# Blocks of 512 rows from the 40th pair on, beside the remaining convolution and routing

## The chip, the core and the metric

The kernel runs on one core of a Trainium2 chip. The metric is the device time of one execution in microseconds (us); less is better. The engines are TensorE (PE, with its weight loads PEld), VectorE (DVE), ScalarE (ACT), GpSimd (POOL) and SyncE (SP). SP and POOL only issue DMAs here, apart from some elementwise work on POOL.

## The reference

A causal convolution of seven taps, whose weights are a softmax per head, feeds a mixture of experts that picks one of eight experts for each row:

```python
w = softmax(weight)                               # 8 heads x 7 taps
y[b, s, c] = sum_k w[head(c), k] * x_padded[b, s + k, c]
logits = y @ w_gate                               # 8 experts
gate = sigmoid(y @ w_local)
for b in range(8):
    for s in range(3584):
        fresh = argmax(logits[b, s])
        e = fresh if s == 0 or gate[b, s] < 0.5 else prev
        prev = e
        p = softmax(logits[b, s])
        out[b, s] = p[e] * (relu(y[b, s] @ w1[e]) @ w2[e])
```

There are 8 x 3584 = 28,672 rows of 192 channels, 8 experts of 1024 hidden units, all in float32.

## The kernel before, in words

The rows are cut into 16 chunks of 1792 rows (`NPART`, `NT` = 14 rows on each of 128 partitions). For each chunk, side work runs in two generators:

- `conv` (L390): per head a first tap on ACT (L401) and six taps on DVE (L411), 8 first taps and 48 DVE instructions for a chunk. The next chunk's x is loaded in its middle.
- `route` (L625) with `logits` (L589): the convolved rows y are transposed on DVE in four instructions (L594), multiplied with the gate weights on PE (L604), copied out of PSUM by ACT (`ls`, L609), transposed back (`lq`, L612) and put in place by 16 small DVE copies (`lt`, L620). Then some seventy small DVE instructions find each row's expert, the probability (with one exp on ACT, L662) and the row's place in a sorted list; `tables` (L778) counts which blocks of 128 rows are full.

After routing, 14 indirect DMAs a chunk, issued by POOL in `put` (L794, the DMA is L801), scatter the rows of the chunk to `slots` in DRAM, sorted by expert. A row carries its probability and its index.

The main work goes over `blocks` (L918): a block is 1, 2 or 4 units of 128 rows of one expert. Before, there are 35 single blocks, 60 pairs (`PAIRED`), then, when all chunks are routed, 13 blocks of 512 rows ("quads"), 4 pairs and 14 singles; a few spare ones run only if they are needed. For each block SP loads the rows (L947) and the expert's weights (L940), three blocks ahead (`AHEAD`).

- A single or pair: `hidden` (L999) multiplies on PE, ACT applies the relu (L1004); `turn` transposes the next block's rows on PE (L383), ACT copies them to xT (L985); `output` multiplies (L1016), ACT scales one half (L1024), DVE adds the other (L1030), and POOL sends the rows out by an indirect DMA (L1034).
- A quad: `seven` (L1136) does the hidden product of 512 rows by 2 x 2 blocks in seven products in place of eight, and four more for the rest (L1152). Its sums are made by `combine_w` on POOL (L1115 to L1121), by `combine_x` on DVE (L1129 to L1133) and by three DVE additions out of PSUM (L1166, L1169, L1179). ACT copies products out of PSUM (L1158, L1161, L1163), applies relu (L1167, L1170, L1180, L1181) and copies the next rows (L1083). `output_late` then has two parts of 256 rows: products (L1196), ACT (L1206), DVE (L1209), POOL (L1214). [...]a quad uses [...]`xps` and three `late_p` tiles, which take the place of the tiles that singles and pairs use.

Every engine executes its instructions in the order in which this program writes them. The order of side work against blocks is set by hand: `step(time)` (L1258) takes instructions from the route and conv generators until their due costs (the numbers that they yield) reach `time`. "hop" ends routing for the step, so that the rest of it goes to the convolution. Steps stand at three places of a pair, with 4.8, 1.2 and 3.6; a quad has none. `ensure` (L1311) loads rows only when their chunk is routed and scattered, and forces steps when a block would come too early.

Of the kernel before, what the change touches and what calls it, by code (L numbers as in the profile page):

```python
# [17 lines left out]
P = 128  # L18
# [4 lines left out]
N = B * S  # L23
# [41 lines left out]
PAIRED = 60  # L65
LEFT4 = E * (QT // 2 + UT // 8)
LEFT2 = E * (BT // 2 + UT // 8)
# [3 lines left out]
PAST = ONE[-1] * UT + TWO[-1] * BT  # L71
FOUR = _likely(N - PAST, QT, LEFT4)
LOST = FOUR - _sure(N - PAST, QT)
# [7 lines left out]
REST = NU - ONE[-1] - 2 * TWO[-1] - 4 * FOUR - 2 * PAIRS + LOSE  # L81
# [21 lines left out]
def kernel(  # L103
# [14 lines left out]
    ys = ctx.enter_context(tc.tile_pool(name="ys", bufs=4))  # L118
# [5 lines left out]
    hp = ctx.enter_context(tc.tile_pool(name="hp", bufs=1))  # L124
    op = ctx.enter_context(tc.tile_pool(name="op", bufs=2))
# [244 lines left out]
    tab = [cst.tile([P, 3], F32, name=f"tab{k}") for k in range(5)]  # L370
    ends = [cst.tile([P, 1 + E], F32, name=f"ends{k}") for k in range(5)]
    for k in range(5):
        nc.gpsimd.memset(tab[k], 0.0)
        nc.gpsimd.memset(ends[k], 0.0)
# [12 lines left out]
    def row_tile():  # L387
        return ys.tile([P, NB, DG], F32, name="y_sb")

    def conv(g, x_sb):  # L390
        y_sb = row_tile()[:, :NT, :]
# [197 lines left out]
    def logits(g, y_sb):  # L589
# [6 lines left out]
        yield "hop"  # L596


        lps = [hps_p.tile([P, TQ * Q], F32, name="hps") for half in range(2)]
# [15 lines left out]
        for r in range(4):  # L615
            for j in range(4):
                t, u = TQ * j, min(TQ * (j + 1), NT)
                at = r // 2 * TQ + t - begin[j]
                e0 = r % 2 * (E + 1)
                nc.vector.tensor_copy(lt[Q * r:Q * r + Q, t:u, :],  # L620
                                      lq[Q * j:Q * j + Q, at:at + u - t, e0:e0 + E + 1])
                yield 0.12
        return lt

    def route(g):  # L625
# [62 lines left out]
        krow = sm.tile([1, 2, P], F32, name="krow")  # L688
# [89 lines left out]
    def tables(g):  # L778
        if ONE[g] > (ONE[g - 1] if g else 0):
            yield from table(0, g, 1, ONE[g])  # L780
        if TWO[g] > (TWO[g - 1] if g else 0):
            yield from table(1, g, 2, TWO[g])
        if g == LAST:
            yield from table(2, g, 4, FOUR, 0)
            yield from table(3, g, 2, PAIRS, 0)
            yield from table(4, g, 1, None)
            yield from fill(g)
# [133 lines left out]
    blocks += [(2, 4, i, LAST) for i in range(FOUR)]  # L921
    blocks += [(3, 2, i, LAST) for i in range(PAIRS)]
    blocks += [(4, 1, i, PADS) for i in range(REST)]
# [40 lines left out]
    def turn(n, xg):  # L964
# [9 lines left out]
        xT = tp.tile([P, KD, BT], F32, name="xT")  # L974
# [69 lines left out]
    def ring(i):  # L1044

        if "rows" not in room:
            room["rows"] = row_tile().rearrange("p b d -> p (b d)")
# [3 lines left out]
    def make_room():  # L1051

        one, two = [xs.tile([P, NX, D], F32, name="x_sb").rearrange("p t d -> p (t d)")
                    for _ in range(2)]
        three = row_tile().rearrange("p b d -> p (b d)")
        for name, flat, at, size in (("xT", one, 0, KD * QT), ("xc", one, KD * QT, 4 * HU * P),
                                     ("wt", one, KD * QT + 4 * HU * P, 6 * P),
                                     ("h0", two, 0, 4 * HU * P), ("h1", two, 4 * HU * P, 4 * HU * P),
                                     ("h2", two, 8 * HU * P, 4 * HU * P), ("h3", three, 0, 4 * HU * P)):
            room[name] = flat[:, at:at + size]  # L1060
# [13 lines left out]
    def turn_in(n, at):  # L1074
        xT = room["xT"][:, :KD * n * P].rearrange("p (d s) -> p d s", d=KD)
# [34 lines left out]
    def combine_w(wb):  # L1110


        wt = room["wt"].rearrange("p (k s) -> p k s", k=3)
        b11, b12, b21, b22 = [wb[:, k * 2 * P:(k + 1) * 2 * P] for k in range(4)]
        nc.gpsimd.tensor_tensor(wt[:, 1, :], b22, b12, op=Alu.subtract)  # L1115
# [3 lines left out]
        nc.gpsimd.tensor_tensor(wt[:, 0, :], b22, b12, op=Alu.subtract)  # L1119
        yield  # L1120
        nc.gpsimd.tensor_tensor(wt[:, 2, :], b21, wt[:, 0, :], op=Alu.subtract)  # L1121
        yield wt

    def combine_x(xT):


        xc = room["xc"].rearrange("p (k s) -> p k s", k=4)
        one, two = slice(0, HU * P), slice(HU * P, KQ * P)
        nc.vector.tensor_tensor(xc[:, 0, :], xT[:, 0, one], xT[:, 0, two], op=Alu.subtract)  # L1129
        nc.vector.tensor_tensor(xT[:, 0, two], xT[:, 0, two], xT[:, 1, two], op=Alu.add)  # L1130
        nc.vector.tensor_tensor(xc[:, 1, :], xT[:, 0, two], xT[:, 0, one], op=Alu.subtract)
        nc.vector.tensor_tensor(xc[:, 2, :], xT[:, 1, one], xc[:, 1, :], op=Alu.subtract)
        nc.vector.tensor_tensor(xc[:, 3, :], xT[:, 2, one], xT[:, 2, two], op=Alu.subtract)  # L1133
        return xc

    def seven(wb, wt, xT, xc, turn_next, weights_next):  # L1136
# [5 lines left out]
        t2, t3, t4 = [wt[:, k, :] for k in range(3)]  # L1142
        a11, s1, a12, a22, a13, a23 = [xT[:, d, s] for d in range(KD) for s in (one, two)]
        s3, s2, s4, s5 = [xc[:, k, :] for k in range(4)]
# [20 lines left out]
        times(wbk, a13, b31)  # L1165
        nc.vector.tensor_tensor(h11, wbk, h11, op=Alu.add)  # L1166
# [17 lines left out]
    def output_late(n, wb, xg, hT, rows_next=None, between=None):  # L1184

        for part, h in enumerate(hT):
# [18 lines left out]
            for k in range(m):  # L1205
                nc.scalar.activation(o_sb[:, k, :], yps[:, 0, k * D:(k + 1) * D], Act.Copy,  # L1206
                                     scale=xg[:, at + k, 0:1])
            for k in range(m):
# [18 lines left out]
    st = {"block": 0, "conv": 1, "cgen": None, "route": 1, "rgen": None, "routed": 1}  # L1227
# [30 lines left out]
    def step(time):  # L1258
# [3 lines left out]
        go = st["rgen"] is not None  # L1262
        while time > 0:
            c = route_op() if go else conv_op()
            if c is None:
                if not go:
                    break
                go = False
            elif c == "hop":
# [3 lines left out]
            else:  # L1273
                time -= c

    ya, yb = row_tile(), row_tile()
    hot = cst.tile([P, 2, NB, UT], F32, name="hot")
# [232 lines left out]
```

## Time and profile before

| | us |
|---|---|
| median of three runs | 1331.99 (1330.92 to 1332.77) |
| the profiled execution's own time | 1305.35 |
| its span, first to last instruction | 1303.6 |
| PE busy | 1284.2 |
| DVE busy | 846.3 |
| ACT busy | 651.1 |
| POOL busy | 523.1 |
| mean granted TensorE clock | 0.997 |

The profile describes one execution; the other times are of executions without it. In the profile a row gives the source line, the engine, the operation, output and inputs by the program's names, and the time that the engine sat idle ahead of it, with what ended that idle time. A name can be that of a tile whose memory was taken over: in quads, `x_sb` and `y_sb` hold hidden values and sums, and block rows.

By its stages the span is: up to about 252 us the start and the singles, then the 60 pairs, from 911 us the 13 quads, from 1176 us the last pairs and singles.

### The profile page before, as it was taken

How to read it: one execution, taken by the hardware profiler on the slowest of the kernel's cores; microseconds unless marked ns; L12 is line 12 of the kernel's file. 1: busy time of each engine (PE TensorE's matmuls, PEld its weight loads, DVE VectorE, ACT ScalarE, POOL GpSimd, SP SyncE). 2: the span in 40 equal slices, each digit the busy share in tenths (PEclk: the TensorE clock that was granted, in tenths of full speed). 3: DMA queues.
4: the chain of work that ended last, by engine and by line, in shares of the span. 5: the costliest groups of instructions: out<-in, count | busy, mean ns of one | idle time of the engine just before them, and what ended most of it. 6: DMA issues, size and time to landing. Idle time of an engine off the chain costs nothing.

```text
span 1303.6 us, 40830 instructions
## 1 busy us (share of the span) xinstructions
PE 1284.2 (99%) x16434; PEld 1220.6 (94%) x16434; DVE 846.3 (65%) x2526; ACT 651.1 (50%) x1482; POOL 523.1 (40%) x577
## 2 busy tenths in 40 slices
PE   9899999999999999999999999999999999999997
PEld 7799999999999999999999999999999999999997
DVE  5989898988988899998999996801333333330000
ACT  5456565544445445444454544444645556454453
POOL 3455353533435344353544534454433433322211
PEclk9999999999999999999999999999999999999999
DMA  5799999975757576575765755666323323324584
GB/s 195 285 357 415 386 384 345 398 273 202 269 203 278 196 274 244 207 280 190 281 246 204 281 193 205 214 213 235 128 87 135 122 105 140 110 94 167 212 303 164
DMA packets 63077, 300.42 MB, mean 230 GB/s; under 512 B 12064, under 2 KB 34263, under 8 KB 45474
## 3 DMA queue, kind: packets, MB, share of 16 engines
q1 hardware_dynamic: 40560, 252.54, 53.2%
q0 software_dynamic: 22320, 45.22, 9.5%
q8 instruction: 131, 2.15, 0.7%
q14 instruction: 64, 0.52, 0.1%
q10 hardware_dynamic: 2, 0.00, 0.0%
HBM read 252.12 MB, written 46.07 MB: 229 GB/s over the span
## 4 chain that ended last, share of the span: by engine, by line
PE 96%; DVE 3%; issue 0%; POOL 0%; POOLq 0%; ACT 0%; DVEq 0%
PE yps L1016 31%; PE hps L999 31%; PE ps L1196 15%; PE ps L1152 8%; PE ps L1103 4%; PE xps L383 2%; PE xps L1152 2%; PE hps L604 2%; DVE y_sb L411 1%; PE hps L233 1%; PE hps L178 0%; DVE hot L574 0%; PE hps L256 0%; PE yps L264 0%; DVE run L475 0%
## 5 line engine op out<-in xcount | busy, mean ns | idle before, releaser
L1016 PE MATMUL yps<-wb,hT 64*128 64x192 f32 x4960 | 429.8, 325 | 3.2 <-DVE o_sb L1030 2.4
L999 PE MATMUL hps<-xT,wb 64*128 64x256 f32 (+1 forms) x4560 | 425.9, 338 | 1.9 <-DVE at L503 1.2
L999 PEld LDWEIGHTS hps<-xT,wb 64*128 64x128 f32 x4560 | 378.7, 188 | 33.9 <-issue 3.9
L1016 PEld LDWEIGHTS yps<-wb,hT 64*128 64x128 f32 x4960 | 405.7, 187 | 4.6 <-DVE o_sb L1030 2.7
L411 DVE SCALAR_TENSOR_TENSOR y_sb<-x_sb,c,y_sb 128x336 f32<-128x336 f32 x672 | 375.6, 569 | 28.4 <-ACT y_sb L401 10.5
L801 POOL DMA_INDIRECT slots<-y_sb,posi x228 | 229.6, 1007 | 205.7 <-ACT xT L985 90.8
L1004 ACT ACTIVATE hT<-hps 128x512 f32<-128x512 f32 (+1 forms) x380 | 176.4, 516 | 244.5 <-PE hps L999 244.5
L1034 POOL DMA_INDIRECT out_dram<-o_sb,xg x155 | 161.5, 1042 | 276.0 <-DVE o_sb L1030 222.2
L1209 DVE SCALAR_TENSOR_TENSOR o_sb<-ps,y_sb,o_sb 128x192 f32<-128x192 f32 x74 | 28.1, 413 | 233.5 <-ACT o_sb L1206 233.5
L1214 POOL DMA_INDIRECT out_dram<-o_sb,y_sb x74 | 76.4, 1032 | 237.5 <-DVE o_sb L1209 218.7
L1196 PE MATMUL ps<-wb,x_sb 64*128 64x192 f32 x1952 | 165.0, 323 | 0.0
L1196 PEld LDWEIGHTS ps<-wb,x_sb 64*128 64x128 f32 x1952 | 159.3, 187 | 0.6
L1024 ACT ACTIVATE o_sb<-yps,xg 128x192 f32<-128x192 f32 x155 | 58.7, 418 | 178.4 <-PE yps L1016 178.3
L985 ACT COPY xT<-xps 128x256 f32<-128x256 f32 (+3 forms) x380 | 142.0, 374 | 10.6 <-PE xps L383 4.8
L1030 DVE SCALAR_TENSOR_TENSOR o_sb<-yps,xg,o_sb 128x192 f32<-128x192 f32 x155 | 58.6, 410 | 77.2 <-ACT o_sb L1024 77.0
L1206 ACT ACTIVATE o_sb<-ps,y_sb 128x192 f32<-128x192 f32 x74 | 27.9, 418 | 102.2 <-PE ps L1196 97.7
L1152 PE MATMUL ps<-x_sb,wb 64*128 64x256 f32 x624 | 73.7, 376 | 0.0
L1152 PEld LDWEIGHTS ps<-x_sb,wb 64*128 64x128 f32 x624 | 59.0, 187 | 7.3
L401 ACT ACTIVATE y_sb<-x_sb,c 128x336 f32<-128x336 f32 x112 | 61.9, 578 | 0.0
L1103 PE MATMUL ps<-x_sb,wb 64*128 64x128 f32 (+1 forms) x864 | 61.6, 295 | 0.0
L1103 PEld LDWEIGHTS ps<-x_sb,wb 64*128 64x128 f32 x864 | 59.4, 188 | 0.9 <-issue 0.2
L1083 ACT COPY x_sb<-xps 128x128 f32<-128x128 f32 (+5 forms) x124 | 58.7, 473 | 2.3
(277 smaller groups left out, 1043.5 us busy)
## 6 DMA issues: line engine op xcount, KB each, us to landing
wb<-in_w_dram SPq DMA_DIRECT2D x122, 1536.0 KB
x_sb<-in_x_dram SPq DMA_DIRECT2D x14, 1920.0 KB
xg<-slots SPq DMA_DIRECT2D x60, 195.0 KB
wb<-in_w_dram SPq DMA_DIRECT2D x12, 512.0 KB
y_sb<-slots SPq DMA_DIRECT2D x13, 390.0 KB
slots<-y_sb,posi POOLq DMA_INDIRECT x228
xg<-slots SPq DMA_DIRECT2D x33, 97.5 KB
x_sb<-in_xb_dram SPq DMA_DIRECT2D x4, 768.0 KB
```

The lines of the kernel that those rows point to most:

```text
L401: nc.scalar.activation(cols(h), chans(h, 0), Act.Copy, scale=c[:, h, 0:1])
L411: nc.vector.scalar_tensor_tensor(cols(h), chans(h, k), c[:, h, k:k + 1], cols(h), Alu.mult, Alu.add)
L801: ins = nc.gpsimd.indirect_dma_start(out=slots[:, :], in_=rows, in_offset=None, out_offset=bass.IndirectOffsetOnAxis(ap=to, axis=0)).ins
L985: copied = nc.scalar.copy(a, b)
L999: nc.tensor.matmul(hps[half][:, j, w], lhsT=wb[rows, f0:f0 + P], rhs=xT[rows, d, w], start=(d == 0 and j == 0), stop=(d == KD - 1), skip_g ...
L1004: relu = nc.scalar.activation(hT[:, m:m + 2, w], hps[half][:, :, w], Act.Relu)
L1016: nc.tensor.matmul(yps[half][:, k * D:(k + 1) * D], lhsT=hT[rows, m, k * P:(k + 1) * P], rhs=wb[rows, WA + m * D:WA + (m + 1) * D], start= ...
L1034: sent = nc.gpsimd.indirect_dma_start(out=out, in_=o_sb[:, k, :], in_offset=None, out_offset=bass.IndirectOffsetOnAxis(ap=xg.bitcast(I32)[ ...
L1103: nc.tensor.matmul(hps[:, half, j, :], lhsT=wb[rows, f0:f0 + P], rhs=xT[rows, d, :], start=(d == 0 and j == 0), stop=(d == KD - 1), skip_g ...
L1152: ins = nc.tensor.matmul(to[:, half, j, :], lhsT=b[rows, j * P:(j + 1) * P], rhs=a[rows, :], start=(first and j == 0), stop=True, skip_gro ...
L1196: ins = nc.tensor.matmul(yps[:, half, k * D:(k + 1) * D], lhsT=h[two][rows, side, j, k * P:(k + 1) * P], rhs=wb[rows, WA + f * D:WA + (f + ...
L1214: sent = nc.gpsimd.indirect_dma_start(out=out, in_=o_sb[:, k, :], in_offset=None, out_offset=bass.IndirectOffsetOnAxis(ap=xg.bitcast(I32)[ ...
```

## The change

Quads begin after the 40th pair. From there on, 18 quads are planned while chunks are still being convolved and routed (`MID`), 5 more come after the last chunk, so there are 35 singles, 40 pairs, 23 quads, 4 pairs and 14 singles. Side work stands in a quad in four parts (`SIDE`): before the first DVE addition (2.4), after the copies of the next rows (4.6) and in the two parts of the output (1.7 and 1.5), between ACT's and DVE's step. What a part overran is taken from the next (`over`), and each routing instruction counts 0.05 more there. The logits products of a chunk, marked by "pe", are written in the first output part of a quad, with a `late_p` tile as PSUM. The 16 small copies `lt` go from DVE to ACT, four to a step.

Memory is dealt out anew, since conv needs its tiles in the stage of quads: hidden values lie in `hot`, small sums in row tiles `xg` and in `hT`; the y tiles of chunk 8 and later rotate over three buffers, and the fourth holds the rows of quads. `combine_x` of the first quad is split, its last two instructions follow the last pair's output. Scatters may also be issued in the second output part of a quad.

```diff
-PAIRED = 60
+NARROW = 8
+PAIRED = 40
 LEFT4 = E * (QT // 2 + UT // 8)
+LEFTM = E * (QT // 2 + UT // 2)
...
+MID = [_likely((g + 1) * PT - PAST, QT, LEFTM) if TWO[g] == TWO[-1] else 0
+       for g in range(LAST)]
...
-    def row_tile():
-        return ys.tile([P, NB, DG], F32, name="y_sb")
+    def row_tile(g):
+        at = g % 4 if g < NARROW else (g + 1) % 3
+        return ys[at].tile([P, NB, DG], F32, name="y_sb")
...
-        yield "hop"
-        lps = [hps_p.tile([P, TQ * Q], F32, name="hps") for half in range(2)]
+        yield "pe"
+        if late_p:
+            both = st["bank"].tile([P, 2, 512], F32, name="ps")
+            lps = [both[:, half, :TQ * Q] for half in range(2)]
+        else:
+            lps = [hps_p.tile([P, TQ * Q], F32, name="hps") for half in range(2)]
...
-                nc.vector.tensor_copy(lt[Q * r:Q * r + Q, t:u, :],
-                                      lq[Q * j:Q * j + Q, at:at + u - t, e0:e0 + E + 1])
-                yield 0.12
+                nc.scalar.copy(lt[Q * r:Q * r + Q, t:u, :],
+                               lq[Q * j:Q * j + Q, at:at + u - t, e0:e0 + E + 1])
+            yield "hop"
...
+        if MID[g] > (MID[g - 1] if g else 0):
+            yield from table(2, g, 4, MID[g], MID[g - 1])
...
+    blocks += [(2, 4, i, next(g for g in range(NPART) if i < MID[g])) for i in range(MID[-1])]
+    blocks += [(3, 4, i, LAST) for i in range(FOUR)]
...
@@ seven @@
         times(wbk, a13, b31)
+        if st["block"] > FIRST:
+            step(SIDE[0], early=1)
         nc.vector.tensor_tensor(h11, wbk, h11, op=Alu.add)
...
@@ output_late @@
+            if n == KQ:
+                step(SIDE[2 + part], late_p[0] if part == 0 else None)
...
+    SIDE = (2.4, 4.6, 1.7, 1.5)
...
-    def step(time):
+    def step(time, bank=None, early=0, force=False):
         start_route()
         start_conv()
         go = st["rgen"] is not None
+        if st["due"]:
+            go = not late_p or bank is not None and (force or st["since"] < st["block"])
+            if go:
+                st["due"], st["bank"] = False, bank
+        time += st["over"]
         while time > 0:
...
+            elif c == "pe":
+                st["due"], st["since"], go = True, st["block"] - early, False
...
-                time -= c
+                time -= c + 0.05 if go and late_p else c
+        st["over"] = min(time, 0) if late_p else 0
...
@@ the main loop @@
                 xc = combine_x(xT)
+                next(xc)
             step(2.4 if i == 0 else 2.1 if n == 1 else 4.8)
             output(n, wbs.pop(i), xgs.pop(i), hT)
...
+            if i == FIRST - 1:
+                more_room()
+                xc = next(xc)
+            if i < FIRST - 1:
+                step(1.3 if n == 1 else 3.6)
...
         if n_next:
             xT, _ = turn_in(n_next, at)
+        if n == KQ:
+            step(SIDE[1])
```

## The prediction, made before the run

> **What bounds the kernel now.** I first read the share of each engine (part 1 of the page), then the stage table. Its columns after the stretch are its length, then busy time of PE, weight loads, DVE, ACT and POOL, then clock, DMA share, GB/s.
>
> ```profile
> PE 1284.2 (99%) x16434; PEld 1220.6 (94%) x16434; DVE 846.3 (65%) x2526; ACT 651.1 (50%) x1482; POOL 523.1 (40%) x577
> ```
> ```profile
> 252.00:911.00 659.00, 659.00 (x8220) 619.35 (x8207) 530.71 (x1680) 313.76 (x711) 289.74 (x284) 1.00 0.67 236
> 911.00:1176.00 265.00, 265.00 (x3010) 249.84 (x3008) 89.08 (x151) 144.58 (x196) 93.24 (x103) 1.00 0.33 115
> ```
>
> PE has no idle time in the stretch of pairs (252 to 911) nor in that of 512-row blocks, "quads" below (911 to 1176). So only less PE work, or a new PE wait, moves the end. Then the chain of waits, which gives the length of a block: start, duration, what.
>
> ```profile
> 846.17 5.18 PE hps L999 x48
> ...
> 899.50 5.18 PE hps L999 x48
> 905.15 5.26 PE yps L1016 x64
> 910.40 3.45 PE ps L1152 x32
> 920.42 10.40 PE ps L1196 x128
> 930.82 3.45 PE ps L1152 x32
> ...
> 1175.62 5.18 PE ps L1103 x48
> ```
>
> Five pairs lie from 846.17 to 899.50: 53.33/5 = 10.67 us each. Thirteen quads lie from 910.40 to 1175.62: 265.22/13 = 20.40 us each. A quad does 11 block products where two pairs do 12; its price is additions on DVE and POOL.
>
> Last, the timeline of one quad (it starts on PE at 1053.16) and of the change from pairs to quads, for the slack of what a quad waits for.
>
> ```profile
> 1054.30 1.01 ACT L1158 COPY x_sb<-ps 128x1024 f32<-128x1024 f32 x1 [0.18 <-PE ps L1152]
> 1055.76 1.03 PE L1152 MATMUL ps<-x_sb 64*128 64x256 f32 x8
> 1058.63 1.23 DVE L1166 TENSOR_TENSOR x_sb<-xps,x_sb 128x1024 f32<-128x1024 f32 x1 [3.74 <-PE xps L1152]
> 1059.77 1.21 DVE L1169 TENSOR_TENSOR y_sb<-ps,y_sb 128x1024 f32<-128x1024 f32 x1
> 1061.40 1.08 PE L1152 MATMUL ps<-x_sb 64*128 64x256 f32 x8
> ```
> ```profile
> 907.87 0.73 POOL L1117 TENSOR_TENSOR wb<-wb 128x256 f32<-128x256 f32 x1
> 907.94 0.94 DVE L1130 TENSOR_TENSOR x_sb<-x_sb 128x256 f32<-128x256 f32 x1 [1.21 <-ACT x_sb L1083]
> 908.92 0.83 DVE L1131 TENSOR_TENSOR x_sb<-x_sb 128x256 f32<-128x256 f32 x1
> 910.24 2.75 PE L1152 MATMUL ps<-x_sb,wb 64*128 64x256 f32 x24
> ```
>
> The copy L1158 ends at 1055.31 and the product that overwrites its PSUM starts at 1055.76: slack 0.45 us. The add L1169 ends at 1060.98, the product into its PSUM starts at 1061.40: slack 0.42 us. DVE waits 3.74 us before L1166; that is where side work must fit.
>
> **What the Trainium skill says.** "SBUF — State Buffer", section "Who interferes with whom": a DVE instruction with two SBUF inputs contends with a GpSimd instruction that reads SBUF. The trace agrees: L1130 and L1131, 0.42 us in their median, took 0.94 and 0.83 us beside the POOL subtractions. "ScalarE: Activation LUTs", section "What ACT_TABLE_LOAD costs": an ACTIVATE takes 186 ns + 0.833 ns per element with immediate operands. The trace agrees roughly (L1158, 1024 elements from PSUM: 1039 ns by this, 1012 measured). No page bears on the rest.
>
> **The change, part by part.**
>
> *Twenty pairs become ten quads.* The table counts agree: 60 pairs and 13 quads before, 40 and 23 after, all else alike. 10 x (2 x 10.67 - 20.40) = 9.3 us less PE work. This is the whole gain.
>
> *Small copies of logits.* 224 copies (L620, mean 190 ns, 42.6 us) leave DVE. On ACT I price one at 186 + 0.833 x 36 = 216 ns by the skill, 48 us in all. In the pairs this gains nothing: PE is full there, 659.00 of 659.00. It costs nothing while ACT's idle 345 us (659 - 314) cover it; a group of four (0.9 us, one per step) stands ahead of the relu L1004, which has over 1 us before L1016 wants it. If the copies had to wait for a late transpose L612, PE could lose up to 1 us per chunk, 12 us in the twelve chunks routed there; I take 0, since L612 follows L609 within 0.6 us in the chunks that I looked at, and keep the 12 for the range. A gain below nothing is excluded by the full PE, apart from the first 250 us, where PE idles for reasons ahead of the first copies.
>
> *Side work beside quads.* By the order of the built program, chunks 14 and 15 are convolved and 13 to 15 routed in blocks 75 to 90; thirteen of these quads carry 8 us or more. A quad's own DVE work is 89.08/13 = 6.9 us of 20.4, the parts allow 10.2, and four POOL subtractions that hit two-input DVE instructions add some 4 x 0.45 = 1.8: 18.9, so it fits in sum. In place, counted from the quad's PE start: the previous output's DVE step L1209 ends at 1.7, the first part (2.4) runs to 4.1, and L1166 can start at 5.47: 1.4 us spare. From L1179's end at 9.2 the second part (4.6) runs to 13.9, with three collisions 15.2; the third (1.7) to 16.9, against 16.0 for L1209; L1209, the five combine_x instructions and the fourth collision end at 20.2, the last part (1.5) at 21.8, L1209 at 22.5 and the next first part at 24.9, before the next L1166 at 25.9. Products want the combine_x results from 21.3. So about 1 us is spare even with every collision, and I take 0.6 us in all for what comes late all the same (a convolution that starts behind ACT's xT copies, exp read by DVE). Bounds: 0, and 1 us in each of thirteen quads.
>
> *ACT in a quad.* The last part's ACT instructions are queued behind the second L1206 and ahead of L1158. L1206 ends at 0.95, L1158 wants 1.14 and has 0.45 us of slack, so 0.6 us is free. One first tap (L401, 0.58) passes. By the built order, the first quad's last part issues four copies and a tap: 0.9 + 0.58 = 1.44, so 0.8 us late on PE; two later ones issue four copies: 0.2 to 0.3 each. I take 1.2 us.
>
> *The change from pairs to quads.* Before, no side work was left there and PE ran on from 905.15 + 5.26 to 910.40 without a gap. Now chunk 13's transposes (L594, 3 x 0.935 + 0.53 = 3.3 us) are queued on DVE behind the first three combine_x instructions, which wait for ACT's xT copies, and its logits products L604 stand on PE right behind the last pair's output. Taken from the trace before, L1131 ends at 909.75; plus 3.3 is 913.05, where PE would be free at 910.24: 2.8 us of PE wait. Also new: the quad's first PSUM tile lies over the tiles of these logits, so PE waits for the two ls copies L609 (0.43 with some 0.2 of latency): 0.6 us. Sum 3.4; bounds 0 (if the transposes run earlier than I think) and 5.
>
> *Moved buffers and queues.* y tiles of chunk 8 and later rotate over three buffers: the first tap on ACT waits for the scatters of the chunk three earlier, with relu L1004 queued behind it. In the built order the last of these scatters is issued about one block (10.7 us) ahead, so 0; up to 1 us if POOL lags. POOL gets scatters beside quads: 7.2 us per quad plus at most ten of 1.0 us, under 20.4, and the subtractions among them are due a quad later. SP: row and weight loads still go out three blocks ahead, none is forced; the x loads of the last chunk now fall beside quads, where the DMA share is 0.33. Cost 0.
>
> Sum: -9.3 + 3.4 + 1.2 + 0.6 = -4.1 us. Against the profiled execution (1305.35 us; its span is 1303.6) that is 1301.2. The shown runs have median 1331.99, 26.6 us above the profiled time, for which the profile has no place; I put the difference on the median: 1327.9.
>
> **Rivals.** (1) *The gain comes whole*: PE runs through the change of stage and the copies are hidden. For it: DVE has spare time in the sum; against it: the order of the queues at the change. -9.3 to -7: 1322.7 to 1325. (2) *DVE becomes the bound of the loaded quads, slower*: the place is L1166/L1169, of which the latter has 0.42 us. If collisions and the small routing instructions put these adds about 1.4 us late, each of thirteen quads loses 1 us: -9.3 + 3.4 + 13 = +7, 1339. It loses against before from 5.9/13 = 0.45 us per quad. For it: L1130 at 0.94 in place of 0.42; against it: 1 us spare after all collisions, and lateness is carried into the next budget. (3) *The pairs pay for ACT's copies*: a late L612 holds the relu and then PE, in twelve chunks by some 0.35 us: 4 us, so no change: 1331.9.
>
> **Chances.** Forecast 0.55, rival (1) 0.20, (2) 0.15, (3) 0.10. About 0.2% (2.7 us) can be told from no change. The forecast's own range is 1325 to 1330.5; four fifths of it (0.44) and all of (1) are faster: 0.64. Same: 0.11 + 0.10 and 0.03 of (2): 0.24. Slower: 0.12. The range from 1322.5 to 1334.5 leaves out most of (2).
>
> **What would show it.** In the profile after: quads of 20.4 us; a PE gap near 3 us ahead of the first quad with DVE L594's successor as releaser; small PE gaps behind L1158's successor; pairs still at 10.67 and no PE idle there. I am wrong if loaded quads run over 20.9 us, if the chunk period of the pairs grows from 55.05 us (first blocks of two chunks at 428.53 and 483.58 in the chain), or if no gap stands at the change.

## The result, and the profile after

The changed kernel took 1340.81 us (median of 7 runs, 1336.93 to 1344.37) against 1331.99 us for the kernel before (7 runs, 1330.92 to 1333.61): ratio 1.0065, 95% interval 1.0046 to 1.0084, slower by 0.65%. The forecast was 1327.9 us. The profiled execution of the changed kernel took 1337.14 us, with a span of 1335.4 us at a granted clock of 0.997.

One fact has to stand ahead of every comparison. In the five comparisons below, the kernel before, unchanged, takes 1305 us in two and 1324 to 1332 us in three, at granted clocks of 0.99 to 1.00 in all of them. The record numbers their chips 15, 14, 8, 13 and 13. The two with number 13 lie twelve minutes apart and have 1331.99 and 1324.67 us for the same kernel, so "a 1305 us chip" below means a chip as it was in one comparison; whether a chip is always quick or slow is not shown. The profile of before that the prediction uses is one of a 1305 us chip: run again on such a chip (run e0_before) it repeats itself stage by stage, and on a 1332 us chip (run d1_before) it does not. The profile of the changed kernel below is one of a slower chip. So the two profiles may not be subtracted; each comparison below stays on one chip or says that it doesn't.

Lines have moved: L999, L1016 and L1004 of before are now L1016, L1033 and L1021; L594, L604, L609, L612, L620 are L603, L617, L622, L625, L633; L1152 is L1173, L1158 is L1179, L1166 and L1169 are L1189 and L1192.

The answer to the first lines shown of before: the share of each engine, and the stretches of singles, of pairs and of quads (columns as in the prediction).

```profile
PE 1294.8 (97%) x16354; PEld 1242.9 (93%) x16354; DVE 890.6 (67%) x2457; ACT 723.9 (54%) x1656; POOL 555.3 (42%) x619
```
```profile
46.00:271.00 225.00, 211.14 (x3325) 201.03 (x3324) 186.55 (x532) 126.96 (x413) 94.64 (x96) 1.00 0.91 346
271.00:726.00 455.00, 447.95 (x5583) 425.98 (x5580) 377.95 (x1130) 243.98 (x609) 191.53 (x188) 1.00 0.67 239
726.00:1206.00 480.00, 475.05 (x5514) 461.28 (x5516) 285.91 (x665) 274.52 (x412) 225.84 (x240) 1.00 0.36 126
...
```

TensorE has 80 matmuls less to do, as planned, but pairs and quads are no longer full: in the profile of before neither had any idle time, now it is 7 us in the pairs and 5 in the quads. The list of waits (engine, line, what it waited for; total us, times, longest) names them:

```profile
PE yps L1033 <- issue: 5.2, 11, 0.9
PE hps L617 <- issue: 4.3, 13, 0.4
PE ps L1173 <- ACT hot L1184: 4.2, 3, 2.4
PE yps L1033 <- ACT hT L1021: 2.4, 4, 1.3
...
PE hps L1016 <- issue: 2.1, 7, 0.5
PE hps L617 <- DVE z L603: 2.1, 3, 1.3
```

Three kinds are seen: gaps that the profile gives no releaser ("issue"; the releaser is what ended the wait), waits for ScalarE (a relu in singles, the copy L1184 in quads), and the wait for the transposes z ahead of the first quad. The last one in the timeline:

```profile
719.32 0.83 DVE L1151 TENSOR_TENSOR xg<-xT 128x256 f32<-128x256 f32 x1
...
720.08 3.14 DVE L603 STREAM_TRANSPOSE z<-y_sb 128x768 f32<-128x768 f32 x4
...
721.19 0.41 PE L617 MATMUL hps<-z,wg 64*32 64x128 f32 x4 [1.29 <-DVE z L603]
...
721.95 0.41 PE L617 MATMUL hps<-z,wg 64*32 64x128 f32 x4 [0.36 <-DVE z L603]
...
722.81 2.72 PE L617 MATMUL hps<-z,wg 64*32 64x128 f32 x88 [0.45 <-DVE z L603]
...
725.56 0.43 ACT L622 COPY ls<-hps 128x128 f32<-128x128 f32 x2 [4.95 <-PE hps L617]
...
726.04 3.44 PE L1173 MATMUL ps<-xT,wb 64*128 64x256 f32 x24 [0.51 <-ACT ls L622]
```

The transposes start where the third addition ends, the logits products follow them one by one, and the first quad waits for the `ls` copy: the order and the releasers that the prediction gave. The second quad shows the other place that it named, small copies and a first tap on ScalarE ahead of L1179:

```profile
748.12 0.90 ACT L633 COPY lt<-lq 32x36 f32<-32x36 f32 x4
749.03 0.58 ACT L410 ACTIVATE y_sb<-x_sb,c 128x336 f32<-128x336 f32 x1
749.52 0.99 ACT L1179 COPY hot<-ps 128x1024 f32<-128x1024 f32 x1
...
750.60 1.14 PE L1173 MATMUL ps<-xg 64*128 64x256 f32 x8 [0.70 <-issue]
```

### The profile page after: what moved, and what is told of

Its sections match the earlier page's. It is cut to its first block, busy times and chain, and to the rows that moved or that the text cites. A ratio compares the mean times of both kernels' runs of the same rounds, so it can differ in the third digit from the quotient of the medians.

```text
span 1335.4 us, 40770 instructions
## 1 busy us (share of the span) xinstructions
PE 1294.8 (97%) x16354; PEld 1242.9 (93%) x16354; DVE 890.6 (67%) x2457; ACT 723.9 (54%) x1656; POOL 555.3 (42%) x619
## 5 line engine op out<-in xcount | busy, mean ns | idle before, releaser
L1033 PE MATMUL yps<-wb,hT 64*128 64x192 f32 x3680 | 328.3, 326 | 10.2 <-issue 5.2
L1016 PE MATMUL hps<-xT,wb 64*128 64x256 f32 (+1 forms) x3600 | 325.2, 329 | 3.7 <-issue 2.1
L1033 PEld LDWEIGHTS yps<-wb,hT 64*128 64x128 f32 x3680 | 304.6, 187 | 17.1 <-issue 11.0
L1016 PEld LDWEIGHTS hps<-xT,wb 64*128 64x128 f32 x3600 | 298.6, 188 | 19.5 <-issue 5.1
L1219 PE MATMUL ps<-wb,hot 64*128 64x192 f32 x3648 | 305.8, 323 | 0.0
L1219 PEld LDWEIGHTS ps<-wb,hot 64*128 64x128 f32 x3648 | 298.4, 187 | 1.2 <-issue 0.8
L1021 ACT ACTIVATE hT<-hps 128x512 f32<-128x512 f32 (+1 forms) x300 | 132.7, 495 | 155.7 <-PE hps L1016 81.4
L1002 ACT COPY xT<-xps 64x256 f32<-64x256 f32 (+4 forms) x300 | 108.1, 360 | 14.9 <-remote 6.7
L1173 PE MATMUL ps<-xT,wb 64*128 64x256 f32 x736 | 88.5, 378 | 0.5 <-ACT ls L622 0.5
L1103 ACT COPY xT<-xps 64x512 f32<-64x512 f32 (+6 forms) x164 | 86.0, 525 | 2.3
L1173 PEld LDWEIGHTS ps<-xT,wb 64*128 64x128 f32 x736 | 75.2, 188 | 4.3 <-ACT ls L622 1.0
L1189 DVE TENSOR_TENSOR hot<-xps,hot 128x1024 f32<-128x1024 f32 x23 | 28.2, 1224 | 59.7 <-PE xps L1173 57.0
L1123 PE MATMUL ps<-xT,wb 64*128 64x128 f32 (+1 forms) x864 | 61.6, 295 | 0.5 <-ACT o_sb L1229 0.5
```

Source lines behind the costliest of these rows:

```text
L1002: copied = nc.scalar.copy(a, b)
L1016: nc.tensor.matmul(hps[half][:, j, w], lhsT=wb[rows, f0:f0 + P], rhs=xT[rows, d, w], start=(d == 0 and j == 0), stop=(d == KD - 1), skip_g ...
L1021: relu = nc.scalar.activation(hT[:, m:m + 2, w], hps[half][:, :, w], Act.Relu)
L1033: nc.tensor.matmul(yps[half][:, k * D:(k + 1) * D], lhsT=hT[rows, m, k * P:(k + 1) * P], rhs=wb[rows, WA + m * D:WA + (m + 1) * D], start= ...
L1103: copied = nc.scalar.copy(a, b)
L1173: ins = nc.tensor.matmul(to[:, half, j, :], lhsT=b[rows, j * P:(j + 1) * P], rhs=a[rows, :], start=(first and j == 0), stop=True, skip_gro ...
```

## The stages on two kinds of chip

Each length is the difference of two starts on TensorE, read in the timeline: the first product L1016 (L999 before), the first of them 256 columns wide (first pair), the first L1173 (L1152), the first L1123 behind the last quad, and the end of the last product.

| execution | singles | pairs | quads | rest |
|---|---|---|---|---|
| before, the profile of the prediction | 207.85 | 657.71 | 265.20 | 119.04 |
| before, e0_before (1305 us chip) | 207.00 | 657.95 | 265.20 | 119.45 |
| changed, a1_after (1305 us chip) | 211.11 | 445.30 | 474.48 | 119.80 |
| before, d1_before (1332 us chip) | 222.49 | 669.26 | 265.40 | 121.53 |
| changed, d2_after (1332 us chip) | 224.15 | 456.65 | 479.44 | 120.16 |
| changed, the profile of the result | 225.51 | 454.72 | 480.47 | 119.80 |

The quads of before, which have no side work, take the same time on both chips. The quads of the changed kernel take 4 to 6 us more on the slower ones; its last eight take 20.2 to 20.5 there too (20.42 in six of them), so the loss lies in those with side work.

## The experiments

There are five comparisons, each on one chip. Theory 1 put the loss at the start of the quads and inside them; theory 2 put it on the small copies on ScalarE, which hold the relu and so TensorE.

**First comparison (before: 1305.43 us).** e0_before is the kernel before.

> The kernel before, unchanged, profiled once more. Theory A (the profiled execution of before, 1305 us, was quicker than its usual 1332, and the waits named 'issue' that the profile after shows on PE in singles and pairs are usual): a profile near 1330 us with some 20 us of PE idle time and stretched blocks ahead of 910 us, and a ratio of 1.000. Theory B (those waits come with the change): a profile near 1305 us with the pairs at 10.67 us throughout, as before.

Measured 1303.81 us, ratio 0.9988 (0.9980 to 0.9996). The quick profile of before repeats itself, so it is not the accident of one execution. Both sides of this ratio are the same kernel: a difference of 1.6 us, outside its own interval, is what two equal kernels can show here, and differences of that size are not read below.

e1_copies is the kernel before with the small copies as the change has them: on ScalarE, in groups of four with a pause ("hop") between them, and with no cost counted in the budget of a step:

```diff
-                nc.vector.tensor_copy(lt[Q * r:Q * r + Q, t:u, :],
-                                      lq[Q * j:Q * j + Q, at:at + u - t, e0:e0 + E + 1])
-                yield 0.12
+                nc.scalar.copy(lt[Q * r:Q * r + Q, t:u, :],
+                               lq[Q * j:Q * j + Q, at:at + u - t, e0:e0 + E + 1])
+            yield "hop"
```

> The kernel before with one part of the change: the 16 small copies per chunk on ScalarE, four to a step. Theory 1 (the loss lies at the start of the quads and inside them): as before, ratio 1.000 within 0.002. Theory 2 (the copies hold ScalarE's relu and xT copies, and so TensorE, in singles and pairs): slower by 5 to 15 us, ratio 1.004 to 1.011.

Measured 1309.56 us, ratio 1.0032 (1.0021 to 1.0043): 4.1 us slower. The singles took 211.40 us in place of 207.00, the pairs 658.80 in place of 657.95. So the copies, issued in this way, cost 4 us, and almost all of it where I had not priced them, in the singles. The largest new wait in its list is for the relu:

```profile
PE yps L1016 <- ACT hT L1004: 2.0, 3, 1.3
```

e2_dve_copies is the changed kernel with the copies as before (VectorE, 0.12 each, no hop).

> The changed kernel with the small copies back on VectorE (0.12 due each, no pause between groups), all else as changed. Theory 1: as the changed kernel within 3 us, ratio 1.004 to 1.009. Theory 2: 5 us or more quicker than the changed kernel, ratio under 1.003.

Measured 1310.54 us, ratio 1.0037 (1.0025 to 1.0049). The singles are back at 207.35, but the first quad took 24.77 us and a later one 30.77, the latter with this wait:

```profile
PE xps L391 <- DVE hot L1189: 7.7, 1, 7.7
```

The long quad carries 59 routing instructions on VectorE, 10.8 us, where the others have at most 42 and 9.3 us. My reading is that the cost counted for the copies delays the routing, until `ensure` must issue a burst of it. The run shows that the way in which the copies are issued makes the loss in the singles; it says nothing on the quads.

e3_quads_late is the changed kernel with all its new buffers, but no quad ahead of the last chunk:

```diff
-PAIRED = 40
+PAIRED = 60
...
-MID = [_likely((g + 1) * PT - PAST, QT, LEFTM) if TWO[g] == TWO[-1] else 0
-       for g in range(LAST)]
-LOST = max([m - _sure((g + 1) * PT - PAST, QT) for g, m in enumerate(MID)])
+MID = [0 for g in range(LAST)]
+LOST = 0
```

> The changed kernel with quads only behind the last chunk: 60 pairs and 13 quads as before, so no side work beside quads; copies on ScalarE, new buffers and split steps stay. Theory 1: as before, ratio 1.000 within 0.003. Theory 2: slower than before by what the copies cost, 5 to 15 us. If the three rotating y tiles hold ScalarE, it is slower than the kernel before with the copies moved.

Measured 1309.59 us, ratio 1.0032 (1.0020 to 1.0044), the same as e1_copies: the moved buffers cost nothing that can be told, as predicted, and the whole loss of this form is that of the copies.

**Second comparison (before: 1304.97 us).** a1_after is the changed kernel.

> The changed kernel as it is, beside the kernel before on one chip, so that block lengths can be compared one by one. Theory 1+2 (ScalarE's small copies hold the singles, +4; the start of the 512-row blocks costs some 4.5; waits inside them the rest): -9.3 + 4 + 4.5 + 7 = +6 to +9 us, ratio near 1.006. Theory C (the loss was the chip's, the reasons of the prediction hold): -4, ratio 0.997.

Measured 1305.11 us, ratio 1.0002 (0.9995 to 1.0008). On this chip the change makes no difference that can be told, which none of the theories had expected. Singles are 4.1 us longer than in e0_before, pairs and quads together 3.4 shorter. Its timeline shows what stands ahead of the relu in a single block:

```profile
197.04 0.42 ACT L1041 ACTIVATE o_sb<-yps,xg 128x192 f32<-128x192 f32 x1 [2.46 <-PE yps L1033]
197.36 0.89 ACT L633 COPY lt<-lq 32x36 f32<-32x36 f32 x4
...
198.26 0.59 ACT L410 ACTIVATE y_sb<-x_sb,c 128x336 f32<-128x336 f32 x1
198.87 0.90 ACT L633 COPY lt<-lq 32x36 f32<-32x36 f32 x4
...
199.79 1.21 ACT L1021 ACTIVATE hT<-hps 128x256 f32<-128x256 f32 x4
200.23 1.93 PEld L1033 LDWEIGHTS yps<-wb,hT 64*128 64x128 f32 x24 [0.59 <-ACT hT L1021]
200.23 2.06 PE L1033 MATMUL yps<-wb,hT 64*128 64x192 f32 x22 [0.43 <-ACT hT L1021]
```

Not one group of four but two, from two parts of the side work that follow each other, and a tap: 2.4 us between the row scaling and the relu. In a single block the products of the hidden values take 2.8 us in place of the 5.3 of a pair, so the first relu is wanted soon. The transpose lq had long been done (L625 ended at 195.06), so it is not what the third rival named.

a2_dve_hop is the changed kernel with `nc.vector.tensor_copy` in place of `nc.scalar.copy` and nothing else: groups, pauses and missing cost stay.

> The changed kernel with the small copies of logits back on VectorE, four to a step as now; all else stays. Theory 1+2: the singles are as before again (-4.4 us against the changed kernel) and a few waits behind ScalarE in the 512-row blocks go (-1 to -2): 5 to 6 us quicker than the changed kernel, ratio to before near 1.002. Theory D (in the singles it is the grouping by fours, not the engine): the singles stay 4 us longer than before.

Measured 1310.67 us, ratio 1.0044 (1.0030 to 1.0059): 5.6 us slower than the changed kernel, a miss. The singles took 214.47 us, longer still, and the wait changed its name:

```profile
PE yps L1033 <- DVE o_sb L1047: 4.9, 7, 2.0
```

In the changed kernel the copies count nothing in the budget of a step, and on VectorE, which is busy 187 of the 207 us of the singles already in e0_before, they then come on top of a full budget. The run also limits what e1 and e2 show. The singles are longer with these groups on either engine, and short where the copies are on VectorE one at a time with their cost counted. A form with the copies on ScalarE and their cost counted was not run, so the engine, the groups and the missing cost are not told apart.

a3_z_early issues the side work of the last pair ahead of `combine_x`:

```diff
             else:
+                step(4.8)
                 wt = list(weights_next())[-1]
                 xT, _ = turn_in(n_next, turn_out(n_next, xgs[i + 1]))
                 xc = combine_x(xT)
                 next(xc)
-            step(2.4 if i == 0 else 2.1 if n == 1 else 4.8)
+            if i < FIRST - 1:
+                step(2.4 if i == 0 else 2.1 if n == 1 else 4.8)
```

> The changed kernel with the side work of the last pair issued ahead of combine_x, so that the transposes z are not queued behind additions that wait for the xT copies; all else stays. Theory 1: the wait of TensorE for z ahead of the first 512-row block (2.1 us plus a gap of 1.3) goes, 3 to 4 us quicker than the changed kernel. Rival: the additions then come late by as much, or the gap moves to the wait for ls: 0 to 1 us quicker.

Measured 1301.91 us, ratio 0.9976 (0.9967 to 0.9986): 3.2 us quicker than the changed kernel, and quicker than the kernel before. The logits products no longer wait, only the `ls` copy is left:

```profile
698.07 1.59 PE L617 MATMUL hps<-z,wg 64*32 64x128 f32 x96
...
699.70 0.43 ACT L622 COPY ls<-hps 128x128 f32<-128x128 f32 x2 [0.79 <-PE hps L617]
700.19 2.00 PE L1173 MATMUL ps<-xT,wb 64*128 64x256 f32 x16 [0.52 <-ACT ls L622]
```

The last pair with the logits took 13.12 us in place of 15.56.

a4_both has both edits.

> The changed kernel with both: small copies on VectorE, side work ahead of combine_x. If the two losses add up: 8 to 10 us quicker than the changed kernel and 1 us quicker than the kernel before, to the same as it (ratio 0.998 to 1.001). If one hides the other: as the better of the two alone.

Measured 1308.44 us, ratio 1.0027 (1.0015 to 1.0038): the edit of a3 is worth 2.2 us here too, and the copies on VectorE without their cost spoil it.

**Third comparison (before: 1324.43 us).** a5_best gives the copies of chunks 2 to 5 back to VectorE with their cost counted, and the pairs a larger step, on top of a3:

```diff
-                nc.scalar.copy(lt[Q * r:Q * r + Q, t:u, :],
-                               lq[Q * j:Q * j + Q, at:at + u - t, e0:e0 + E + 1])
-            yield "hop"
+                src = lq[Q * j:Q * j + Q, at:at + u - t, e0:e0 + E + 1]
+                if g <= 5:
+                    nc.vector.tensor_copy(lt[Q * r:Q * r + Q, t:u, :], src)
+                    yield 0.12
+                else:
+                    nc.scalar.copy(lt[Q * r:Q * r + Q, t:u, :], src)
+            if g > 5:
+                yield "hop"
...
-                step(2.4 if i == 0 else 2.1 if n == 1 else 4.8)
+                step(2.4 if i == 0 else 2.1 if n == 1 else 5.4)
```

> The changed kernel with the side work of the last pair ahead of combine_x, and with the small copies of chunks 2 to 5 back on VectorE one at a time with their cost counted (steps of the pairs 5.4 in place of 4.8, so that no routing is forced later); later chunks stay on ScalarE. If the copies on ScalarE cost 4 us in the stage of single blocks and nothing behind it, and the start of the 512-row blocks 3: singles 207 us in place of 211, in all 6 to 7 us quicker than the changed kernel; ratio to before 0.995. If the copies cost as much on VectorE: as with the side work ahead of combine_x alone, ratio 0.9976.

Measured 1344.80 us, ratio 1.0166 (1.0149 to 1.0183), a clear miss. The singles were 6.0 us shorter than in c5_after_again (214.34 against 220.36), but the pairs 19.9 longer (472.51 against 452.64). The parts of a pair now add to 5.4 + 1.2 + 3.6 = 10.2 us, with the 0.74 of the row scaling 10.9, more than the 10.67 of a pair on TensorE; that this is the cause is argued from the sum, and that the next form without it (d3) loses nothing in the pairs agrees.

c4_spread leaves the copies of chunks 2 to 5 on ScalarE, one group every second step:

```diff
             yield "hop"
+            if g <= 5:
+                yield "hop"
```

> The changed kernel, small copies of chunks 2 to 5 still on ScalarE, but a group of four only every second step, so that no two groups stand between the row scaling of one block and the relu of the next. If it is ScalarE's time ahead of the relu that holds TensorE in the singles: two thirds of the 4 us come back (singles 208 to 209 us, ratio to before 0.997 to 0.998). If it is a late transpose lq, as the third rival of the prediction has it, or the engine change as such: singles stay at 211, ratio as the changed kernel's.

Measured 1335.03 us, ratio 1.0086 (1.0073 to 1.0099), singles 223.24: slower than the changed kernel. No wait for a relu is left in its list, but gaps named "issue" at L617 grew from 2.5 to 4.9 us. This speaks against the relu as the whole cause, but other gaps came with the edit.

c5_after_again is the changed kernel.

> The changed kernel once more, beside the kernel before, for whether the ratio belongs to the kernel or to the chip. On a chip on which the kernel before takes some 1305 us: ratio 0.9995 to 1.001 as before. On one on which it takes some 1332 us: 1.005 to 1.008. If the ratio wanders on the same kind of chip, the first measurement was the odd one.

Measured 1329.95 us, ratio 1.0050 (1.0032 to 1.0067), where a1_after had 1.0002 (0.9995 to 1.0008). The ratio of the same two kernels changes with the comparison.

**Fourth comparison (before: 1331.99 us).** d1_before and d2_after are the two kernels.

> The kernel before, unchanged, for its profile on the chip of this comparison. On a chip on which it takes some 1305 us: pairs of 10.67, spans of stages as in the profile of before. On one on which it takes 1320 us or more: theory S (the slower chips stop ScalarE and TensorE for 1 to 2 us at fixed places of the program, and what follows decides what that costs) has it lose in singles and pairs by less per stage than the changed kernel does, and little in its thirteen 512-row blocks, which have no side work; theory U (a slower chip slows both kernels alike) has equal losses in singles and pairs, and the ratio near 1.000.

> The changed kernel, unchanged, to be set stage by stage against the kernel before on the same chip. Chip of 1305 us: ratio 0.9995 to 1.001. Chip of 1320 us or more: 1.004 to 1.008, of which theory S puts 4 us on the singles (as on the quick chip), 4 on the start of the 512-row blocks, 3 to 6 on waits inside these.

Measured 1332.33 us, ratio 1.0010 (1.0000 to 1.0021), and 1339.72 us, ratio 1.0078 (1.0056 to 1.0101). This is the result once more, with both profiles from one chip. The stretch of quads of d1_before, then of d2_after:

```profile
938.00:1204.00 266.00, 266.00 (x3019) 265.48 (x3017) 90.29 (x153) 144.94 (x196) 93.89 (x104) 1.00 0.33 115
```
```profile
727.00:1207.00 480.00, 475.06 (x5522) 458.17 (x5524) 287.04 (x667) 274.73 (x414) 225.80 (x240) 1.00 0.36 127
```

The thirteen quads of before have no idle time, the twenty-three of the changed kernel have 5 us. What the idle time is, is seen where the same instruction is laid side by side on two chips, here in the fourth quad. First the profile of the result, then a1_after:

```profile
790.08 1.01 ACT L1179 COPY hot<-ps 128x1024 f32<-128x1024 f32 x1 [0.19 <-PE ps L1173]
...
791.51 1.06 PE L1173 MATMUL ps<-xg 64*128 64x256 f32 x8
...
792.38 1.92 PE L1173 MATMUL xps<-xT,wb 64*128 64x256 f32 x16
...
794.73 1.01 ACT L1182 COPY hot<-ps 128x1024 f32<-128x1024 f32 x1 [3.64 <-PE xps L1173]
795.02 1.22 DVE L1189 TENSOR_TENSOR hot<-xps,hot 128x1024 f32<-128x1024 f32 x1 [2.82 <-PE xps L1173]
...
796.71 1.13 PE L1173 MATMUL ps<-xg 64*128 64x256 f32 x8 [2.41 <-ACT hot L1184]
```
```profile
763.80 1.01 ACT L1179 COPY hot<-ps 128x1024 f32<-128x1024 f32 x1 [0.19 <-PE ps L1173]
...
765.24 1.06 PE L1173 MATMUL ps<-xg 64*128 64x256 f32 x8
...
765.52 1.01 ACT L1182 COPY hot<-ps 128x1024 f32<-128x1024 f32 x1 [0.71 <-PE ps L1173]
...
767.83 1.06 PE L1173 MATMUL ps<-xg 64*128 64x256 f32 x8
```

The copy L1182 starts 0.7 us behind the end of the one before it on the quick chip and 3.6 us behind it on the slower one. Nothing that runs on ScalarE lies between. The same instruction is late in all three profiles of the changed kernel on slower chips (idle ahead of it 3.64, 2.22 and 2.97 us).

ScalarE is not what stops there. L1182 waits for a semaphore (a counter by which one engine tells another that it is done) that TensorE raises, and the trace holds the times at which it was raised. By TensorE's own records four products end at 791.71, 792.58, 793.44 and 794.30; their semaphore was raised at 794.65, 794.74, 794.84 and 794.93, in one burst, and ScalarE's wait ended 0.02 us after the first. In a1_after the same four were raised within 0.02 us of the products' ends. The addition L1189 on VectorE waits for the same semaphore. The late signal holds L1182 and L1184, and the next product waits for L1184. In d2_after the fourth, tenth and fifteenth quads take 22.46, 21.04 and 22.48 us, each behind such late signals, where a1_after has 20.41 to 20.42: together 4.7 us, nearly the whole difference between their quads.

All profiles divide in this way. Of some 940 to 960 such signals of TensorE, 15 to 44 have no semaphore time within 0.1 us of the product's end in the nine profiles near 1305 us, and 239 to 325 in the eleven slower ones. (The counts are rough: the slower traces lack some of the semaphore records, and the ends of products are modelled.) In d1_before these are 131 of 252 in the singles and 183 of 440 in the pairs, but 2 of 131 in the quads, which have no side work; in the quads of d2_after they are 44 of 252. Of the 25 semaphore times there that lie away from every product's end, 22 fall in the first fifteen quads, the ones with side work. So the late signals go with the side work, and the change brings them into the quads. Why they come late is not shown.

The two profiled executions lie 3.5 us above and 1.8 us below their medians, so they show 2.1 of the 7.4 us between these; which stage has the rest I can't say.

The edits of d3_early_dve on top of a3_z_early are the copies as in a5_best, with the step of the pairs left at 4.8, and

```diff
-    SIDE = (2.4, 4.6, 1.7, 1.5)
+    SIDE = (2.4, 4.8, 1.7, 1.5)
...
-                if j > i + 2:
+                if j > i + (1 if late_p else 2):
```

> The changed kernel with side work of the last pair ahead of combine_x, the small copies of chunks 2 to 5 on VectorE with their cost counted, steps of the pairs as they are (4.8), second part of the side work 4.8 in place of 4.6, and rows of a 512-row block asked for one block ahead at the latest, so that no routing is forced. If the two causes add (4 us in singles, 3 at the start of the 512-row blocks): 6 to 7 us quicker than the changed kernel; on a chip of 1305 us ratio to before 0.995. If the copies cost as much on VectorE: 3 us quicker, 0.9976.

Measured 1327.23 us, ratio 0.9971 (0.9958 to 0.9983): 12.5 us quicker than the changed kernel, twice what was expected, and 5 us quicker than the kernel before. In the profiles the singles are 3.6 us shorter than in d2_after, the pairs 7.4 shorter, the quads 4.5 longer (one more chunk has its logits in them, 1.7). The run has four edits at once, so the gain is that of all of them. It was not run on a 1305 us chip.

d4_spread is c4_spread again.

> Once more the changed kernel with a group of small copies only every second step for chunks 2 to 5, since on the chip of the first trial the waits for the relu went but other gaps came. On a chip of 1305 us: if ScalarE's time ahead of the relu holds TensorE, singles of 208 to 209 us in place of 211; if not, 211 or more.

Measured 1338.38 us, ratio 1.0066 (1.0046 to 1.0086), singles 222.33 against 224.15. Not to be told from the changed kernel.

**Fifth comparison (before: 1324.67 us).** f1_hold keeps all copies on ScalarE and moves those of chunks 2 to 5 to where it waits for TensorE:

```diff
         for r in range(4):
+            if g <= 5 and r % 2 == 0:
+                yield "hold"
...
-            yield "hop"
+            if g > 5:
+                yield "hop"
...
-        go = st["rgen"] is not None
+        go = st["rgen"] is not None and (mid or force or not st["hold"])
+        st["hold"] = st["hold"] and not go
...
+            elif c == "hold":
+                st["hold"], go = True, False
...
-                if j > i + 2:
+                if j > i + (1 if late_p else 2):
...
-            step(2.4 if i == 0 else 2.1 if n == 1 else 4.8)
+            step(2.4 if i == 0 else 2.1 if n == 1 else 4.8, mid=True)
```

f2_hold_z has the edit of a3_z_early as well, f3_early_dve is d3_early_dve again.

> The changed kernel, all small copies on ScalarE, but those of chunks 2 to 5 only in the part of the side work that is issued between the xT copies and the row scaling of a block, where ScalarE waits for TensorE anyway, eight at a time (rows of a 512-row block asked for one block ahead at the latest, so that no routing is forced). If the relu behind the copies is what TensorE waits for in the singles: 3 to 4 us quicker than the changed kernel there (on a chip of 1305 us singles of 207 to 208, ratio 0.997; on one of 1332 us ratio 1.004). If it isn't: singles as the changed kernel's, ratio 1.000 or 1.0075.

> The same with the side work of the last pair ahead of combine_x. If both causes hold and add: another 3 us, ratio 0.995 on a chip of 1305 us and 1.001 on one of 1332 us. If the first doesn't hold: 0.9976 and 1.005.

> Once more the kernel with the small copies of chunks 2 to 5 on VectorE and the early side work, on whichever chip this is: 0.995 on a chip of 1305 us if its gain is that of the two causes (4 and 3 us), 0.997 as measured on one of 1332 us.

Measured in this order: 1339.56 us, ratio 1.0109 (1.0085 to 1.0132); 1336.64 us, ratio 1.0094 (1.0069 to 1.0118); 1319.49 us, ratio 0.9957 (0.9939 to 0.9976). The first two are misses: in f1_hold the singles took 223.12 us, the waits for the relu are gone, and this one is in their place:

```profile
PE yps L1036 <- DVE o_sb L1050: 6.6, 7, 2.1
```

While the routing is held, the steps fill up with convolution, nine VectorE instructions of 0.59 us in a block of 5.44, and the addition L1050 on VectorE comes late. So here too a change in where the copies stand changes what the rest of the step is filled with. The third run repeats d3 in another comparison; its singles took 216.72 us, 6.4 less than those of f1_hold.

## Why the prediction was wrong

*Gain of 9.3 us.* Right. Undisturbed pairs and quads of a1_after take 10.67 and 20.42 us: 10 x (2 x 10.67 - 20.42) = 9.2.

*Small copies, "I take 0".* This step failed on the quick chip, and it is all that failed there: 4.1 us by e1_copies in place of 0. The price of one copy was right: 215 ns in their mean (L633, 224 of them, 48.1 us) against the estimate of 216 ns from what the Trainium skill says of an ACTIVATE ("ScalarE: Activation LUTs", section "What ACT_TABLE_LOAD costs"). What failed is the sentence that made it cost nothing, "It costs nothing while ACT's idle 345 us cover it": these were the pairs' idle time, and there it held (0.85 us in 60 pairs). The twelve chunks were a slip: fourteen have such copies, and in a1_after three have them in the singles, a fourth across their end, seven in the pairs and three beside quads. The stage of the singles I had dismissed as one "where PE idles for reasons ahead of the first copies"; between the copies of two chunks its blocks run at 5.44 us each without a gap. A group there stands ahead of a relu with half the room, and two groups stand together. That the copies as the change issues them make the 4 us is shown (e1, e3, and e2 where they are issued as before). Which part of that does it, the engine, the groups or the missing cost, is not (a2 loses more on VectorE); nor is it that the relu makes all of it, since waits for it sum to 2.0 us, and c4, d4 and f1 took them away without gain.

*Side work in quads and ScalarE, 0.6 + 1.2 us.* Right on the chip that the profile was from: the quads of a1_after take 474.48 us; 22 x 20.42 + 20.18 = 469.4 without disturbance, and two chunks' logits are 3.4 (12.28 + 10.77 - 2 x 10.67 = 1.71 each), which leaves 1.6. The largest piece, 0.94 us, is the quad named, the second; how the sum splits into the two terms was not tried. On the 1332 us chip the same sum gives 479.44 - 469.4 - 3.4 = 6.6: 5 us more, behind late signals of TensorE, which the quads of before hardly have (2 of 131 in d1_before). The second rival, VectorE as the bound, did not occur.

*Change from pairs to quads, 3.4 us.* Right in place, order and size on the quick chip: the last pair took 15.56 us there; less 10.90 as in e0_before and 1.71 for the logits, 2.95 remain, and a3_z_early gives 3.2 us by taking the cause away. On the 1332 us chip the same difference is 17.22 - 10.91 - 1.71 = 4.6 (10.91 in d1_before), and in the profile of the result 17.96 - 10.91 - 1.71 = 5.3, above the bound of 5.

*Moved buffers, 0.* Right (e3_quads_late against e1_copies: 0.03 us apart).

*From the profile to the median.* This is the second step that failed, and on the chip of the result the larger one: "26.6 us above the profiled time, for which the profile has no place; I put the difference on the median." These 26.6 us are the distance between a 1305 us and a 1332 us chip, on which TensorE's signals come late, and a difference between two kernels does not carry over: it is +0.1 us on the quick chip (a1_after) and +5.5 to +8.8 on the slower ones (c5_after_again, d2_after and the result). On the quick chip the sum -9.2 + 4.1 + 1.6 + 3.0 is -0.5, plus 0.85 for the pairs; measured is +0.1 (1305.11 against 1304.97). On a 1332 us chip, 5 us in the quads and 1.6 at the change come on top, near the 7.4 to 8.8 us measured there. This closes only roughly, since the singles of the two kernels differ by 1.7 us in the one pair of profiles from that chip, not by 4.1.

So the direction was lost by the copies and by the chip together: with the copies where they were in the singles and the transposes ahead of the additions (d3, f3), the form with quads beside side work is 0.3 to 0.4% quicker than the kernel before on the slower chips.

## What to carry to other kernels

A small operation that is moved to a less busy engine has to be priced in the stage with the least slack, not in the one where most of the operations lie, and by what it stands ahead of in that engine's queue. A budget that no longer counts a moved operation fills up with other work, so the engine that was to be relieved can stay as full. When a copy waits, look for when its semaphore was raised before putting the stop on the copy's engine. Before a profile and a median are set against each other, ask whether they come from one chip: 1.000 and 1.008 are both ratios of the same two kernels, with intervals that do not meet.

## What the runs showed of the hardware

- The same program, unchanged, took 1303.81 to 1305.43 us, 1324.43 to 1324.67 us and 1331.99 to 1332.33 us in different comparisons, with granted clocks of 0.99 to 1.00. The clock in the records doesn't tell these apart.
- What does tell them apart is when TensorE's signals come: 15 to 44 of them away from the product's end in each profile near 1305 us, 239 to 325 in each slower one. The burst in the fourth quad makes the copy L1182 late by 1.5 to 2.9 us more than on the quick chip.
- On the slower chips the logits products in the singles have gaps of some 0.2 to 0.5 us with no releaser: three of the four chunks take 4.1 to 4.8 us in d1_before against 1.6 to 1.9 in e0_before, while in the pairs they run through in 1.59 us on a slower chip too. What makes these gaps was not tried.
